# First 192 rows' local scaling shared by two engines, and a new searched order table

## The chip, the cores and the metric

One core of one Trainium2 chip runs one program that holds the whole chain. The metric is the device time in microseconds, the median of several executions. Lower is better.

## What is computed

The input has 4 batches of 8 heads, 576 rows and 64 columns. Attention is the sum of two parts, each a softmax of its own: one over means of 4 rows, repeated back to full length, and one over neighbours less than 4 rows away. Its output, as 2304 rows of 512, goes through two experts.

```
out_up = repeat(softmax(q_d k_d^T / 8) v_d, 4)         # q_d, k_d, v_d: means of 4 rows
attn   = out_up + softmax(where(|i-j| < 4, q k^T / 8, -1e9)) v
h = x @ w_in;  x1 = (max(h, 0) + alpha * min(h, 0)) @ w_out        # 512 -> 2048 -> 512
xn = x1 / rms(x1) * rms_g
out = (silu(xn @ w_gate) * (xn @ w_val)) @ w_out2                  # 512 -> 1536 -> 512
```

Both softmaxes divide by their sum plus 1e-9. All is fp32.

## The kernel before, in words

The large products take fp32 apart into a high and a low fp16 half and add three fp16 products on TensorE. The weights therefore go through a chain before use: a DMA on the SP queue brings a raw piece (L1143, L1153), ScalarE and VectorE decode it (`Piece.decode`, L1162, L1165, L1167, L1170, L1171), TensorE squares it (`sqps`, L1183), VectorE takes the sum of squares (L1184), TensorE adds it over the partitions (`allps`, L391), a few small VectorE steps make a power of two as scale (L404 to L408), and `split` writes the high half on ScalarE (L415) and the low half on VectorE (L416). For `w_in` the two halves stand in the tile `wi`; it comes in six pieces.

Batch 0's first 384 rows are computed by the class `Dense`, on blocks of 96 rows (i, two of them) and 96 + 6 keys, for two halves of a head pair (j). Per pair of lanes `local` has these steps: scores on TensorE (`lsps`, L920 to L932), maxima on VectorE (L938), in `s1` exponentials with their row sums on ScalarE (L952, one instruction for each i and j, 96 x 102), in `s2` the inverse of the sums on VectorE (L958, L959) and the scaling of the exponentials (L967 on ScalarE for the first 192 rows, c = 0; GpSimd for the others, `self.big(c)`), in `s3` transposes on TensorE (`ltps`, L976) and their eviction on ScalarE (L978), in `s4` the products with v (`lops`, L988), the sum with the pooled part on VectorE (L997) and the split into `xt`. The pooled attention's steps in `down` are transposes `tps` (L844), their eviction `T` (L845), scores `sps`, exponentials `dd` (L877) and products `avps`.

The first expert for these rows is `m1_first`. It calls `h_mm` (L1416) for two column blocks of 128 at a time: 24 matmuls of 128 x 192 into one PSUM tile `hps`. There are two such buffers (`ps_w`, tag "w"). To empty one, ScalarE takes the negative part (L1420, tile `g`), VectorE adds it with its factor (L1422, twice), ScalarE writes the high half of the result (L415, tile `g0`), and VectorE the low half (L416). Only then is the buffer free for the next but one product. `hps_835`, `hps_921` and `hps_1008` are the first three.

```
        nc.scalar.activation(out=g, in_=ps, func=AF.Relu, scale=-1.0)
        for j in range(fs):
            nc.vector.scalar_tensor_tensor(out=ps[:, j], in0=g[:, j], scalar=oma[:, f + j:f + j + 1], in1=ps[:, j],
                                           op0=ALU.mult, op1=ALU.add)
```

The order on each engine is not that of the code. `issue_order` (from L72) is called last. It records all instructions with estimated costs (`cost`, `transfer`, `lag`), takes a list scheduler back and forth over them for 40 rounds, and keeps the best round's priorities. To these it adds the table `LEADS` (L24): each entry shifts the priorities of a range of instruction numbers by some ns. One more pass of the scheduler gives the sequence of every engine, which is then pinned as it stands. Its forward pass has a model of TensorE's clock: in stretches in which TensorE did little in the stretch before, its matmuls take about twice as long (`slow`). SP's DMA issues are an engine like the others there, so its queue is ordered by the same pass.

Of the kernel before, what the change touches and what calls it, by code (L numbers as in the profile page):

```python
# [12 lines left out]
AF = mybir.ActivationFunctionType  # L13
ALU = mybir.AluOpType
# [4 lines left out]
def view(ap, dims, off=0, parts=None):  # L19
# [2 lines left out]


LEADS = (  # L24
# [28 lines left out]
)  # L53


def issue_order(tc, nc, groups, rounds=40):
# [53 lines left out]
    def transfer(o, i):  # L110
        sides = [[c for _, c in a.ap if c > 1] or [1] for a in (o, i)]
        rings = max(x for x in range(1, 17) if not any(s[0] % x for s in sides))
        n = max(runs(a)[0] for a in (o, i))
        each = 4.0 * min(runs(a)[1] for a in (o, i))
        share = n / 16 * (10.0 + 0.046 * each)
        return max(share, n / rings * (9.0 + 0.042 * each)), max(share, 600.0)

    def cost(k, ins, outs):
        i, e = insts[k], eng[k]
# [61 lines left out]
    for k, (ins, outs) in enumerate(aps):  # L181
        for l, wr in ((ins, False), (outs, True)):
            for a in l:
                n = a.tensor.name
# [46 lines left out]
    def lag(a, b):  # L231
        return 2300 if eng[a] == "SP" else waits.get((eng[a], eng[b]), 100)
# [7 lines left out]
    def run(P, S, prio, fwd, d):  # L240
# [9 lines left out]
        for _ in count:  # L250
            t, e = min((clock[e] if now[e] else max(clock[e], soon[e][0][0]), e) for e in engines if now[e] or soon[e])
            while soon[e] and soon[e][0][0] <= t:
                k = heapq.heappop(soon[e])[1]
                heapq.heappush(now[e], (prio[k], k))
            k = heapq.heappop(now[e])[1]
            if fwd and e == "PE":
                while t >= (win + 1) * WIN:
                    slow, win, done = done < BUSY, win + 1, 0
                done += work[k]
                real[k] = (2 * d[k] - 2.5 if slow else d[k]) + fixed[k]  # L260
            if fwd and shared[k]:
                real[k] += max(0.0, port - t)
                port = t + real[k]
            end[k] = t + real[k]
            clock[e] = end[k] if held[k] is None else t + held[k]
            seq[e].append(k)
            for s in S[k]:
                left[s] -= 1
                at[s] = max(at[s], end[k] + (lag(k, s) if fwd else lag(s, k)))
                if not left[s]:  # L270
                    if fwd and mate.get(k) == s:
                        heapq.heappush(now[e], (-1e30, s))
                    else:
                        heapq.heappush(soon[eng[s]], (at[s], s))
# [22 lines left out]
def kernel(  # L297
# [14 lines left out]
    nc = tc.nc  # L312
# [458 lines left out]
    class Dense:  # L771
# [141 lines left out]
        def local(self, c, h0, banks):  # L913
# [42 lines left out]
            def s2():  # L956
# [3 lines left out]
                for n, s in enumerate(ls["s"]):  # L960
# [2 lines left out]
                                                op=ALU.mult)  # L963
                        continue
                    for i in range(QC):
                        for j in range(2):
                            nc.scalar.activation(out=s[:, i, j], in_=s[:, i, j], func=AF.Copy,  # L967
                                                 scale=sm[:, n, i, j:j + 1])

            def s3():  # L970
                ls["t"] = []
# [819 lines left out]
```

## Time and profile before

| | us |
|---|---|
| median of 3 runs (lowest, highest) | 958.61 (958.48, 958.99) |
| profiled execution | 958.69 |
| its span | 957.0 |
| TensorE (PE) busy | 928.3 (97%) |
| VectorE (DVE) busy | 676.8 (71%) |
| ScalarE (ACT) busy | 481.4 (50%) |
| GpSimd (POOL) busy | 128.0 (13%) |

The span reaches from the first to the last instruction that the profiler saw; the execution's own time has 1.7 us around it. Busy is the time in which an engine's instructions ran; TensorE's loading of weights (PEld) lies beside its matmuls. An arrow in a row names what the engine waited for: `[0.73 <-DVE g L416]` is idle time of 0.73 us before the instruction, ended by VectorE's work on tile g at line 416. Names of tiles carry a number only in the listings of the order.

### The profile page before, as it was taken

Reading aid. Unit: us, or ns where it says so; the run is one execution under the profiler, and the core shown is the slowest. Engines: PE = TensorE matmul, PEld = TensorE weight load, DVE = VectorE, ACT = ScalarE, POOL = GpSimd, SP = SyncE. Lnnn points to the kernel's source line nnn. Section 1 sums busy time; section 2 is a strip of 40 time slices with the busy share of each in tenths; the row PEclk is TensorE's granted clock in tenths of the full one; section 3 lists DMA queues with packets and bytes.
Section 4 is the critical chain, followed back from the end, with each engine's and each line's share of the span. In section 5 each row is a group of like instructions: output and inputs, shape, how many; then the busy total and the mean of one; then the engine's idle time right before and its main releaser. Section 6 shows DMA issues by size and latency. Waiting matters only on the chain.

```text
span 957.0 us, 16449 instructions
## 1 busy us (share of the span) xinstructions
PE 928.3 (97%) x6484; PEld 599.6 (63%) x6484; DVE 676.8 (71%) x1333; ACT 481.4 (50%) x1108; POOL 128.0 (13%) x103
## 2 busy tenths in 40 slices
PE   6978999999999999999999999999999999999998
PEld 5667877799555565556666655555566666555554
DVE  4789996899999968999977899973333342442333
ACT  5899989889872472233576322222332433221322
POOL 1101100211022003332102323220000000000000
PEclk9999999999999999999999999999999999999999
DMA  9976444574221241121032120200000000000000
GB/s 214 278 253 177 130 143 130 196 234 137 72 74 58 91 150 50 55 78 55 25 88 84 50 65 20 50 18 1 23 12 1 1 2 1 1 1 12 23 1 34
DMA packets 53711, 73.79 MB, mean 77 GB/s; under 512 B 22190, under 2 KB 35138, under 8 KB 53634
## 3 DMA queue, kind: packets, MB, share of 16 engines
q1 hardware_dynamic: 53634, 72.74, 25.3%
q8 instruction: 51, 0.84, 0.4%
q14 instruction: 26, 0.21, 0.1%
HBM read 68.01 MB, written 4.72 MB: 76 GB/s over the span
## 4 chain that ended last, share of the span: by engine, by line
PE 78%; ACT 4%; DMA 3%; DVE 3%; issue 1%; SPq 0%; ACTq 0%
PE gps L1533 26%; PE acc L1433 16%; PE hps L1416 16%; PE oacc L1562 14%; DMA out_dram<-ob 3%; PE avps L749 1%; PE sps L709 1%; PE atps L737 1%; DMA wr<-in_moe_w_gate_dram 1%; ACT wr L1165 1%; ACT w L415 1%; DVE prod L575 1%; PE xps L612 1%; DVE hps L1422 1%; DVE wc L1167 0%
## 5 line engine op out<-in xcount | busy, mean ns | idle before, releaser
L1416 PE MATMUL hps<-xt,wi 128*128 128x192 f16 (+1 forms) x1536 | 345.9, 289 | 6.6 <-DVE g L416 4.3
L1533 PE MATMUL gps<-x,w 128*128 128x384 f16 x1728 | 349.5, 326 | 0.6 <-ACT x L1447 0.4
L1433 PE MATMUL acc<-ghl,wo 128*128 128x384 f16 (+1 forms) x960 | 249.4, 310 | 0.5 <-ACT ghl L415 0.4
L1533 PEld LDWEIGHTS <-w 128*128 128x128 f16 x1728 | 169.4, 98 | 116.5 <-issue 2.6
L1562 PE MATMUL oacc<-w,uhl 128*128 128x512 f16 x630 | 200.4, 379 | 1.8 <-ACT ob L1618 1.7
L1416 PEld LDWEIGHTS <-wi 128*128 128x128 f16 x1536 | 148.0, 100 | 59.3 <-issue 7.7
L1433 PEld LDWEIGHTS <-wo 128*128 128x128 f16 x1344 | 128.8, 99 | 60.0 <-issue 2.6
L1422 DVE SCALAR_TENSOR_TENSOR hps<-g,oma,hps 128x192 f32<-128x192 f32 (+1 forms) x128 | 66.1, 517 | 66.1 <-ACT g L1420 65.4
L1542 ACT ACTIVATE th<-gps,tsc 128x384 f32<-128x384 f32 x72 | 41.7, 581 | 124.2 <-PE gps L1533 123.9
L1562 PEld LDWEIGHTS <-uhl 128*128 128x128 f16 x630 | 61.8, 98 | 64.3 <-issue 2.5
L1544 DVE SCALAR_TENSOR_TENSOR th<-th,gps 128x384 f32<-128x384 f32 x72 | 39.6, 551 | 84.9 <-ACT th L1542 84.7
L1553 ACT ACTIVATE uhl<-gps 128x384 f16<-128x384 f32 x72 | 41.7, 579 | 107.0 <-DVE gps L1547 98.5
L1420 ACT ACTIVATE g<-hps 128x384 f32<-128x384 f32 x96 | 47.0, 489 | 95.7 <-PE hps L1416 95.4
L521 POOL TENSOR_TENSOR prod<-cq,ckv 128x896 f32<-128x896 f32 x24 | 53.1, 2213 | 172.9 <-DVE ls L532 52.2
L1433 PE MATMUL acc<-g,wo 128*128 128x384 f16 (+1 forms) x384 | 69.8, 286 | 0.0
L1554 DVE TENSOR_TENSOR uhl<-gps,uhl 128x384 f16<-128x384 f32 x72 | 45.4, 630 | 28.4 <-ACT uhl L1553 28.1
L575 POOL TENSOR_TENSOR prod<-ls,ckv 128x896 f32<-128x896 f32 x24 | 47.9, 1997 | 126.4 <-issue 54.8
L416 DVE SCALAR_TENSOR_TENSOR ghl<-hps,grp,ghl 128x384 f16<-128x384 f32 (+1 forms) x73 | 44.3, 608 | 27.0 <-ACT ghl L415 26.7
L415 ACT ACTIVATE ghl<-hps,grp 128x384 f16<-128x384 f32 (+1 forms) x73 | 41.9, 574 | 40.2 <-DVE hps L1422 37.2
L532 DVE TENSOR_REDUCE ls<-prod 128x14 f32<-128x896 f32 x48 | 51.0, 1076 | 0.0
L1162 ACT ACTIVATE wr<-wr 128x768 f32<-128x768 f32 (+1 forms) x48 | 41.5, 874 | 8.7 <-DMA wr<-in_moe_w_val_dram 4.9
L1547 DVE SCALAR_TENSOR_TENSOR gps<-th,kap,gps 128x384 f32<-128x384 f32 x60 | 37.1, 618 | 9.6 <-PE gps L1533 7.0
(240 smaller groups left out, 1143.4 us busy)
## 6 DMA issues: line engine op xcount, KB each, us to landing
wr<-in_moe_w_out_dram SPq DMA_DIRECT2D x18, 512.0 KB
wr<-in_moe_w_in_dram SPq DMA_DIRECT2D x10, 768.0 KB
wr<-in_moe_w_gate_dram SPq DMA_DIRECT2D x8, 768.0 KB
wr<-in_moe_w_val_dram SPq DMA_DIRECT2D x8, 768.0 KB
ckv<-in_k_dram SPq DMA_DIRECT2D x7, 768.0 KB
ckv<-in_v_dram SPq DMA_DIRECT2D x7, 768.0 KB
wr<-in_moe_w_out_dram SPq DMA_DIRECT2D x20, 256.0 KB
sd<-in_q_dram SPq DMA_DIRECT2D x24, 144.0 KB
```

The source lines that it names most:

```text
L415: nc.scalar.activation(out=hi, in_=src, func=AF.Copy, scale=s)
L416: nc.vector.scalar_tensor_tensor(out=lo, in0=src, scalar=s, in1=hi, op0=ALU.mult, op1=ALU.subtract)
L521: engs[i].tensor_tensor(out=pr, in0=view(st["q"][:, j, t:t + TP], [[D, TP], [0, ND], [1, D]]), in1=view(st["k"][:, j, t:t + TP], [[D, TP], ...
L532: nc.vector.tensor_reduce(out=st["s"][:, j, t:t + TP], in_=st.pop(("p", i)), axis=AX.X, op=ALU.add)
L575: engs[i].tensor_tensor(out=over(pr, i), in0=view(st["s"][:, j, t:t + TP], [[ND, TP], [1, ND], [0, D]]), in1=view(st["v"][:, j, t:t + TP], ...
L1416: nc.tensor.matmul(ps[:, j], wi[:, f + j, a, kk * 128:(kk + 1) * 128], x[:, b_, kk, c0:c0 + n], start=(i == 0), stop=(i == 3 * KK - 1))
L1420: nc.scalar.activation(out=g, in_=ps, func=AF.Relu, scale=-1.0)
L1422: nc.vector.scalar_tensor_tensor(out=ps[:, j], in0=g[:, j], scalar=oma[:, f + j:f + j + 1], in1=ps[:, j], op0=ALU.mult, op1=ALU.add)
L1433: nc.tensor.matmul(acc[e], wo_f(f)[:, a, e * 128:(e + 1) * 128], hl[:, b_], start=(f == f0 and i == 0), stop=(f == f1 and i == 2))
L1533: nc.tensor.matmul(ps, w2_t[i0 + f // 3].rearrange("p a (k c) -> p a k c", k=KK)[:, a, kk, (f % 3) * 128:(f % 3 + 1) * 128], xh[:, b_, kk] ...
L1554: nc.vector.tensor_tensor(out=t1, in0=vp, in1=t0, op=ALU.subtract)
L1562: nc.tensor.matmul(acc[tt], t[:, a, tt * 128:(tt + 1) * 128], w[:, b_, f % 3], start=(f in first and i == 0), stop=(f in last and i == 2))
```

## The change

Three parts. In `s2` the first 192 rows' exponentials were scaled by ScalarE alone, 16 instructions of 96 x 102; now j = 0 stays on ScalarE and j = 1 is scaled by VectorE. In the planner, a transfer of at most 16 runs costs at least 3000 ns in its model, and in its slow stretches a matmul that finds TensorE idle costs 90 ns more and its followers on other engines come 100 ns later. And the table `LEADS` holds other entries, three rows fewer (its first row before and now is shown). Lines of the changed kernel from L256 on stand up to 4 lower or higher than before; the scalings are L967 and L968, and other lines named below are one higher from there on (L1420 is L1421).

```
 LEADS = (
-    (6142, 6149, 8500), (4634, 4657, 4000), (1841, 1850, 500), (2437, 2444, -500), (1116, 1482, 1000), (6896, 6972, -500),
...
+    (6142, 6149, 8500), (5545, 5548, 22500), (2175, 2183, 4500), (493, 561, -3000), (3639, 3651, -19500), (450, 467, -3500),
...
@@ -113,7 +110,7 @@
         n = max(runs(a)[0] for a in (o, i))
         each = 4.0 * min(runs(a)[1] for a in (o, i))
         share = n / 16 * (10.0 + 0.046 * each)
-        return max(share, n / rings * (9.0 + 0.042 * each)), max(share, 600.0)
+        return max(share, n / rings * (9.0 + 0.042 * each), 3000.0 if n <= 16 else 0.0), max(share, 600.0)
 
     def cost(k, ins, outs):
         i, e = insts[k], eng[k]
@@ -253,11 +250,15 @@
                 k = heapq.heappop(soon[e])[1]
                 heapq.heappush(now[e], (prio[k], k))
             k = heapq.heappop(now[e])[1]
+            late = 0.0
             if fwd and e == "PE":
                 while t >= (win + 1) * WIN:
                     slow, win, done = done < BUSY, win + 1, 0
                 done += work[k]
                 real[k] = (2 * d[k] - 2.5 if slow else d[k]) + fixed[k]
+                if slow:
+                    real[k] += 90.0 if t > clock[e] else 0.0
+                    late = 100.0
             if fwd and shared[k]:
                 real[k] += max(0.0, port - t)
                 port = t + real[k]
@@ -266,7 +267,7 @@
             seq[e].append(k)
             for s in S[k]:
                 left[s] -= 1
-                at[s] = max(at[s], end[k] + (lag(k, s) if fwd else lag(s, k)))
+                at[s] = max(at[s], end[k] + late + (lag(k, s) if fwd else lag(s, k)))
                 if not left[s]:
                     if fwd and mate.get(k) == s:
                         heapq.heappush(now[e], (-1e30, s))
@@ -963,9 +964,9 @@
                                                 op=ALU.mult)
                         continue
                     for i in range(QC):
-                        for j in range(2):
-                            nc.scalar.activation(out=s[:, i, j], in_=s[:, i, j], func=AF.Copy,
-                                                 scale=sm[:, n, i, j:j + 1])
+                        nc.scalar.activation(out=s[:, i, 0], in_=s[:, i, 0], func=AF.Copy, scale=sm[:, n, i, 0:1])
+                        nc.vector.tensor_scalar(out=s[:, i, 1], in0=s[:, i, 1], scalar1=sm[:, n, i, 1:2],
+                                                scalar2=None, op0=ALU.mult)
 
             def s3():
                 ls["t"] = []
```

Three places of the order. The first is the scaling of the first lanes. On ScalarE it stood thus before (`dls` are the exponentials, `dlsum` the sums; `dd` are exponentials of the pooled part):

```order
L877 ACTIVATE dd_334,dsum_344<-sps_337,dm_343 72x144
L877 ACTIVATE dd_334,dsum_344<-sps_338,dm_343 72x144
L877 ACTIVATE dd_334,dsum_344<-sps_337,dm_343 72x144
L877 ACTIVATE dd_334,dsum_344<-sps_338,dm_343 72x144
L967 ACTIVATE dls_414<-dls_414,dlsum_411 96x102 x2
L967 ACTIVATE dls_419<-dls_419,dlsum_411 96x102 x2
L1165 ACTIVATE wr_665<-wr_665,nhalf_99 128x768
L845 ACTIVATE T0_200<-tps_363 128x288
```

and stands thus with the change:

```order
L878 ACTIVATE dd_334,dsum_344<-sps_338,dm_343 72x144
L1166 ACTIVATE wr_690<-wr_690,nhalf_99 128x768
L878 ACTIVATE dd_334,dsum_344<-sps_337,dm_343 72x144
L967 ACTIVATE dls_414<-dls_414,dlsum_411 96x102
L878 ACTIVATE dd_334,dsum_344<-sps_338,dm_343 72x144
L967 ACTIVATE dls_419<-dls_419,dlsum_411 96x102
L967 ACTIVATE dls_414<-dls_414,dlsum_411 96x102
L967 ACTIVATE dls_419<-dls_419,dlsum_411 96x102
```

with this on VectorE:

```order
L862 TENSOR_TENSOR dd_316<-sdv_160 72x256
L960 RECIPROCAL dlsum_411<-dlsum_411 96x8
L650 SCALAR_TENSOR_TENSOR vqps_236,vm_225<-vqps_236,ident_97 128x128
L968 TENSOR_SCALAR dls_414<-dls_414,dlsum_411 96x102
L968 TENSOR_SCALAR dls_419<-dls_419,dlsum_411 96x102
L968 TENSOR_SCALAR dls_414<-dls_414,dlsum_411 96x102
L968 TENSOR_SCALAR dls_419<-dls_419,dlsum_411 96x102
L860 TENSOR_TENSOR sdv_166<-sdv_166 72x4x128
```

The four scalings of j = 1 are a row on VectorE, right behind the inverse of the sums, between sums of squares and the pooled means of v (`sdv`, `dd`).

The second is ScalarE's queue up to the first high halves (`g0_834<-hps_835`). Before, with nine weight splits in a row:

```order
L1162 ACTIVATE wr_768<-wr_768 128x768
L415 ACTIVATE wi_107<-wc_662,swi_113 128x512 x3
L415 ACTIVATE wi_107<-wc_687,swi_113 128x512 x3
L415 ACTIVATE wi_107<-wc_712,swi_113 128x512 x3
L1162 ACTIVATE wr_1108<-wr_1108 128x768
L1420 ACTIVATE g_860<-hps_835 128x384
L1165 ACTIVATE wr_1108<-wr_1108,nhalf_99 128x768
L1420 ACTIVATE g_946<-hps_921 128x384
L1162 ACTIVATE wr_770<-wr_770 128x768
L415 ACTIVATE g0_834<-hps_835,sc_105 128x2x192
```

With the change:

```order
L416 ACTIVATE wi_107<-wc_687,swi_113 128x512 x2
L1163 ACTIVATE wr_1184<-wr_1184 128x768
L416 ACTIVATE wi_107<-wc_712,swi_113 128x512
L1166 ACTIVATE wr_1184<-wr_1184,nhalf_99 128x768
L416 ACTIVATE wi_107<-wc_742,swi_113 128x512 x2
L1421 ACTIVATE g_860<-hps_835 128x384
L416 ACTIVATE wi_107<-wc_767,swi_113 128x512
L416 ACTIVATE wi_107<-wc_742,swi_113 128x512
L1421 ACTIVATE g_946<-hps_921 128x384
L416 ACTIVATE g0_834<-hps_835,sc_105 128x2x192
```

The same instruction is row 110 before and row 137 with the change (a row may stand for several), and pieces of the weights from 742 and 767, which before were decoded and split behind it, are split in front of it.

The third is SP's queue of loads, near its start. Before:

```order
L1143 DMA wr_665<-in_moe_w_in_dram 128x2x768
L795 DMA wo_108<-in_q_dram 96x6x64
L803 DMA sdv_166<-in_v_dram 72x2x512
L795 DMA wo_108<-in_k_dram 96x6x64
L803 DMA sdv_172<-in_v_dram 72x2x512
L803 DMA sdv_174<-in_v_dram 72x2x512
L795 DMA wo_108<-in_q_dram 96x6x64
L795 DMA wo_108<-in_k_dram 96x6x64
```

With the change:

```order
L796 DMA wo_108<-in_k_dram 96x6x64
L804 DMA sdv_160<-in_v_dram 72x2x512
L796 DMA wo_108<-in_k_dram 96x6x64
L1144 DMA wr_665<-in_moe_w_in_dram 128x2x768
L796 DMA wo_108<-in_q_dram 96x6x64
L1696 DMA rows_176<-in_moe_alpha_dram 16x128
L1696 DMA rows_176<-in_moe2_rms_g_dram 4x128
L796 DMA wo_108<-in_q_dram 96x6x64
L796 DMA wo_108<-in_k_dram 96x6x64
L1144 DMA wr_688<-in_moe_w_in_dram 128x2x768
```

The loads of the third head's q and k (`wo` from `in_q` and `in_k`, in the second half of these pieces) stand ahead of three loads of v (`sdv_166`, `sdv_172`, `sdv_174`), and the second and third weight pieces (`wr_665`, `wr_688`) have fewer loads ahead of them.

## Rows read from the trace of the kernel before

**Rows 1.** The page: its head and part 1, busy time by engine.
```profile
span 957.0 us, 16449 instructions
...
PE 928.3 (97%) x6484; PEld 599.6 (63%) x6484; DVE 676.8 (71%) x1333; ACT 481.4 (50%) x1108; POOL 128.0 (13%) x103
```

**Rows 2.** Busy time by stretch: start:end length, engines, granted clock, DMA share, GB/s.
```profile
0.00:40.00 40.00, 30.89 (x197) 23.52 (x197) 23.28 (x74) 26.71 (x83) 5.82 (x30) 1.00 1.00 248
40.00:80.00 40.00, 33.86 (x286) 27.00 (x283) 33.33 (x79) 37.87 (x103) 1.46 (x2) 0.91 0.80 264
80.00:120.00 40.00, 36.53 (x448) 31.15 (x445) 38.15 (x107) 37.80 (x114) 8.09 (x12) 1.00 0.44 119
120.00:160.00 40.00, 40.00 (x400) 31.38 (x398) 33.27 (x87) 36.68 (x94) 0.00 (x0) 1.00 0.45 130
...
240.00:250.00 10.00, 7.95 (x61) 5.46 (x61) 9.08 (x17) 7.77 (x11) 1.84 (x1) 1.00 0.15 50
```

**Rows 3.** Busy time by stretch: columns PE, PEld, DVE, ACT, POOL as above.
```profile
0.00:21.10 21.10, 13.38 (x76) 9.73 (x77) 9.36 (x37) 10.08 (x35) 3.23 (x28) 1.00 0.95 209
...
0.00:71.60 71.60, 57.72 (x412) 44.08 (x413) 49.65 (x131) 56.19 (x154) 7.10 (x31) 0.98 0.89 248
...
72.30:107.70 35.40, 31.68 (x375) 27.82 (x375) 33.14 (x93) 33.20 (x101) 3.99 (x8) 0.95 0.57 156
```

**Rows 4.** TensorE's waits, 0 to 120 us: us in total, times, longest.
```profile
PE hps L1416 <- DVE g L416: 4.3, 4, 2.5
```

**Rows 5.** Timeline of TensorE: start, us, line, operation, tiles, shape, count, idle before.
```profile
72.30 0.90 PE L1416 MATMUL hps<-xt,wi 128*128 128x192 f16 x9 [2.47 <-DVE g L416]
...
105.43 1.40 PE L1416 MATMUL hps<-xt,wi 128*128 128x192 f16 x15 [0.73 <-DVE g L416]
...
107.40 2.90 PE L1416 MATMUL hps<-xt,wi 128*128 128x192 f16 x33
```

**Rows 6.** Timeline of ScalarE, first high halves.
```profile
71.02 0.57 ACT L415 ACTIVATE g<-hps,sc 128x384 f16<-128x384 f32 x1
```

**Rows 7.** Timeline of VectorE, first and ninth low halves.
```profile
71.62 0.62 DVE L416 SCALAR_TENSOR_TENSOR g<-hps,sc,g 128x384 f16<-128x384 f32 x1
...
107.05 0.61 DVE L416 SCALAR_TENSOR_TENSOR g<-hps,sc,g 128x384 f16<-128x384 f32 x1
```

**Rows 8.** Timeline of ScalarE, two exponentials of one row and four scalings.
```profile
19.01 0.33 ACT L952 ACTIVATE dls<-lsps,dlm 96x102 f32<-96x102 f32 x1
...
19.33 0.33 ACT L952 ACTIVATE dls<-lsps,dlm 96x102 f32<-96x102 f32 x1
...
24.46 1.20 ACT L967 ACTIVATE dls<-dls,dlsum 96x102 f32<-96x102 f32 x4
```

**Rows 9.** Groups of ScalarE, 0 to 71.6 us, shapes apart: count, busy us, mean ns, idle.
```profile
L1162 ACT ACTIVATE wr<-wr 128x768 f32<-128x768 f32 x15 | 13.5, 905 | 1.9 <-DMA wr<-in_moe_w_in_dram 1.7
L1165 ACT ACTIVATE wr<-wr,nhalf 128x768 int32<-128x768 uint32 x9 | 8.9, 991 | 0.0
...
L415 ACT ACTIVATE wi<-wc,swi 128x512 f16<-128x512 f32 x9 | 5.6, 709 | 0.3 <-DVE swi L406 0.3
L967 ACT ACTIVATE dls<-dls,dlsum 96x102 f32<-96x102 f32 x16 | 5.4, 381 | 0.0
...
L978 ACT ACTIVATE laT<-ltps 102x384 f32<-102x384 f32 x4 | 1.9, 485 | 0.0
...
L1162 ACT ACTIVATE wr<-wr 128x256 f32<-128x256 f32 x1 | 0.4, 434 | 0.0
```

**Rows 10.** Groups of VectorE, 0 to 107.7 us, shapes apart.
```profile
L1170 DVE TENSOR_SCALAR wc<-wr 128x768 int32<-128x768 int32 x6 | 3.3, 549 | 1.4 <-ACT wr L1162 1.4
...
L1170 DVE TENSOR_SCALAR wc<-wr 128x256 int32<-128x256 int32 x2 | 0.6, 292 | 0.3 <-ACT wr L1162 0.3
```

**Rows 11.** Busy time by stretch: columns as above, the granted clock third from last.
```profile
66.00:67.00 1.00, 1.00 (x8) 0.92 (x7) 1.00 (x3) 1.00 (x3) 0.00 (x0) 0.50 1.03 365
...
76.00:77.00 1.00, 1.00 (x9) 0.95 (x7) 1.00 (x3) 1.00 (x8) 0.00 (x0) 0.50 1.03 321
```

More of the change, by code (lines that the diff above doesn't have):

```diff
@@ L115, in transfer @@
         share = n / 16 * (10.0 + 0.046 * each)
-        return max(share, n / rings * (9.0 + 0.042 * each)), max(share, 600.0)
+        return max(share, n / rings * (9.0 + 0.042 * each), 3000.0 if n <= 16 else 0.0), max(share, 600.0)
     def cost(k, ins, outs):
@@ L255, in run @@
             k = heapq.heappop(now[e])[1]
+            late = 0.0
             if fwd and e == "PE":
@@ L260, in run @@
                 real[k] = (2 * d[k] - 2.5 if slow else d[k]) + fixed[k]
+                if slow:
+                    real[k] += 90.0 if t > clock[e] else 0.0
+                    late = 100.0
             if fwd and shared[k]:
@@ L268, in run @@
                 left[s] -= 1
-                at[s] = max(at[s], end[k] + (lag(k, s) if fwd else lag(s, k)))
+                at[s] = max(at[s], end[k] + late + (lag(k, s) if fwd else lag(s, k)))
                 if not left[s]:
@@ L965, in s2 @@
                     for i in range(QC):
-                        for j in range(2):
-                            nc.scalar.activation(out=s[:, i, j], in_=s[:, i, j], func=AF.Copy,
-                                                 scale=sm[:, n, i, j:j + 1])
+                        nc.scalar.activation(out=s[:, i, 0], in_=s[:, i, 0], func=AF.Copy, scale=sm[:, n, i, 0:1])
+                        nc.vector.tensor_scalar(out=s[:, i, 1], in0=s[:, i, 1], scalar1=sm[:, n, i, 1:2],
+                                                scalar2=None, op0=ALU.mult)
             def s3():
```

53 rows, old and new, of the table LEADS are left out of this document.

## The prediction

> **What bounds the kernel now.** I read the page's head, then the busy time by stretch, then what the engines wait for in the first 120 us, and last the single rows around the first expert's h products. TensorE is busy for 928.3 of 957.0 us [rows 1], so at most 28.7 us can be had from waits, and the stretches say where they lie. The three of 40 us up to 120 us hold 30.89, 33.86 and 36.53 us of TensorE work, which leaves 9.1 + 6.1 + 3.5 = 18.7 us idle; from 120 to 160 us nothing is idle, and the 10 us from 240 on hold 7.95, so 2.05 are lost there [rows 2]. The change touches none of the matmuls' sizes and its moves end at some 320 us. So it works on these 20.8 us.
>
> In the head the weights and the attention of batch 0 are made ready together. ScalarE is then busy for 56.19 of the first 71.60 us, idle for 15.4, and 11.0 of that idle time had passed by 21.10 us (10.08 busy), while TensorE waited for its inputs [rows 3]. From then on ScalarE works almost without a gap, in a fixed order. What TensorE waits for most often once the h products begin is the release of their PSUM buffers: 4.3 us in 4 waits [rows 4]. There are two such buffers; the third product waits 2.47 us, to 72.30, for the first pair's values, and later ones 0.73 us [rows 5]. The values come out by way of ScalarE, then VectorE: the high halves of the first product start on ScalarE at 71.02 [rows 6], the low halves on VectorE at 71.62, done at 72.2; the ninth product's low halves start at 107.05 and are done at 107.7 [rows 7], and tile hps_1514, the eleventh product, reuses that buffer. It starts some 0.1 us later, within the run of 33 matmuls from 107.40 [rows 5]. Between the two low halves VectorE is busy for 33.14 of 35.40 us [rows 3]. So two queues in series set when TensorE gets on here: ScalarE up to the first high half, VectorE from there to the ninth low half.
>
> **The change, part by part.**
>
> *Scalings.* Of 16 on ScalarE, 8 stay and 8 go to VectorE. Four in a row take 1.20 us [rows 8], 0.38 of it one alone [rows 9], so each costs 0.27 by its distance to the next: 8 x 0.27 = 2.2 us less for ScalarE. VectorE's price for 96x102 is not in the trace. Its nearest rows are the same kind of operation on 256 elements, 0.292 us, and on 768, 0.549 [rows 10]; the smaller width can cost no more than the first and no less than nothing beyond its fixed part, which a line through both puts at 0.292 - 256 x 0.0005 = 0.16. I take 0.22, on that line, so 8 x 0.22 = 1.8 us, bounds 1.3 to 2.3. VectorE is idle for 71.6 - 49.65 = 22.0 us ahead of the first product's values [rows 3], and that covers it. The Trainium skill (VectorE: DVE Perf Modes, Mode 2×_2P) says that a one-source fp32 operation from SBUF to SBUF reads through both ports and yields two results a cycle; the slope between the two rows, 0.0005 us an element, agrees with it.
>
> *ScalarE ahead of the first high halves.* The new order puts 142 instructions ahead of them where 122 stood. By kind, at the distance from one to the next (an instruction's recorded time less the some 0.11 us by which it overlaps its follower): 16 more exponentials at 0.32 [rows 8] = 5.1; 4 more weight splits at 0.61 = 2.4; 2 more decodings of 768 at 0.80 and 2 of 256 at 0.32 = 2.2; 2 more of the other decoding at 0.88 = 1.8; 2 more evictions of transposes at 0.37 = 0.7 [rows 9]; 8 fewer scalings, -2.2. Sum 10.0 us, so 56.2 + 10.0 = 66.2 us of ScalarE work in place of 56.2. Its idle time has a floor of 11.0 us, already past by 21.10 us [rows 3]; loads that come earlier (the third head's keys, the second weight piece) can lower the 4.4 us that came later, and weight pieces wanted earlier than their loads can raise it, by 1.9 us if the last one is waited for. I take 15.4, as it was. The first high halves are then done at 66.2 + 15.4 = 81.6 and the low halves 0.6 later, at 82.2 instead of 72.2: 10.0 us later. VectorE is not the later one: its rows ahead of that point rise by some 9 us, to 59 us of work, with 22 us to spare.
>
> *VectorE from the first to the ninth low half.* 87 rows stand there where 83 stood. Five decoding steps, two joinings of the output weights, two weight splits and three square sums go out; adds and reductions of the pooled attention and two sums of the local one come in; by the durations in the trace both weigh the same, 33.2 and 33.3 us. With 0 to 2.3 us of idle time (2.3 before), taken at 1.1, hps_1514 starts at 82.2 + 33.3 + 1.1 = 116.6 in place of 107.8: 8.8 us later.
>
> *TensorE's work ahead of it.* More of it is done by then: 16 transposes, 16 local products, 8 of the pooled attention's squares, 8 transposes and 4 products of it, 4 of h, 2 of the output. At the distances in the trace (0.09, 0.06, 0.07, 0.09, 0.15, 0.085, 0.16 us) that is 5 us, and 5.5 with the slower spacing where kinds alternate. So of 8.8 us 5.5 are paid back: +3.3 us.
>
> *Clock.* Before shows whole microseconds at 0.50 of the full clock, 1.2 of 2.4 GHz, while h products run [rows 11]; there are two such stretches of 3.4 us, each costing 1.7 us of TensorE. While the two queues above set the time, the clock costs nothing beyond what they allow, and I put it at nothing. Later TensorE does not stand long enough to show a fall in the rows of before.
>
> *Queues.* GpSimd's order is untouched. On SP the loads of the third head pass three loads of v, and weight pieces move ahead; the effect is in the idle time above. The 2.05 us at 240 us [rows 2] rest on an order that changes too; between nothing and all of it can go, and I take 1.0.
>
> *Sum.* +3.3 - 1.0 = +2.3 us. The profiled execution took 958.69 (span 957.0 and 1.7 around it), which is 0.1 over the median of the three runs. 958.7 + 2.3 = 961.0.
>
> *Ends.* Low: ScalarE idle 13.0, no idle time on VectorE, all of 2.05 back: 79.8 + 33.3 = 113.1, +5.3 - 5.5 - 2.05 = -2.3, so 956.4. High: idle 17.3, VectorE idle 2.3, nothing back: 84.1 + 35.6 = 119.7, +11.9 - 5.5 = +6.4, so 965.1.
>
> **The rivals.**
>
> *Faster: the head's loads decide, not the queues.* If the reordered loads take away ScalarE's late idle time down to the floor of 11.0 us, the first low halves are done at 77.8 and hps_1514 at 111.1: +3.3 - 5.5 = -2.2, and with the wait at 240 us gone, -4.3: 954.4 to 956.5. It decides from an idle time of some 13 us downwards. For it: 4.4 us of waiting after 21 us, and the third head's loads moved up. Against it: the weight pieces are wanted earlier too, from the same DMA.
>
> *No change.* The added work ahead is the same work that came behind, and TensorE uses the wait: with ScalarE idle at 14 us and no idle time on VectorE the sum is 80.8 + 33.3 = 114.1, +6.3 - 5.5 - 1.0 = -0.2: 958.5. The scaling's 2.2 us are in it. That the shared scaling alone changes nothing is part of this case: it frees ScalarE inside a chain that other work fills.
>
> *Slower by more: the clock falls again.* TensorE now waits longer ahead of the first buffers, and twice the clock has been at 0.50 beside such a wait [rows 5, 11]. If after hps_1514, where TensorE is the bound again, two more such stretches follow, 2 x 1.7 us are added: 964.4. The Trainium skill (TensorE: Matmul & The Clock Gate, A second HAM failure mode: psum-queue depth-cycling) describes the same: small idle spells between groups of matmuls as PSUM buffers go round make the clock swing; it speaks against an order that bunches the waits. The half-clock rows of before agree with it, but after 80 us the clock reads 1.00 [rows 2].
>
> **How the numbers follow.** A measurement of this kernel can tell about 0.2%, 1.9 us, from no change. The forecast of about 961 I give 0.38, the clock rival 0.10, no change 0.28, faster 0.24. The forecast's own range is 960.0 to 963.5. Slower by over 1.9 us: 0.38 + 0.10 = 0.48; within: 0.28; faster: 0.24. The range for 8 in 10 goes from 956.0 to 965.1: it leaves out some two thirds of the faster case and the end of the clock case.
>
> **What would show it.** Right: first high halves on ScalarE near 81 us, first low halves near 82, the ninth's near 116; ScalarE's idle time up to there near 15.4; eight scalings of 0.2 to 0.3 us on VectorE within time it had free; nothing idle on TensorE from 120 to 160 us. Wrong: first low halves before 79 us, or hps_1514 before 113, or waits gone after 160 us by more than 2 us; then the gain came from loads or from later stages that this sum holds still.

## The result, and the profile after

| | before | changed |
|---|---|---|
| median of 6 runs, us (lowest, highest) | 959.74 (958.48, 961.64) | 967.74 (966.77, 969.87) |
| ratio to before, 95% interval | | 1.0083 [1.0063, 1.0103] |
| profiled execution, us (span) | 958.69 (957.0) | 967.33 (965.6) |
| TensorE idle, 0 to 160 us | 18.7 | 21.9 |
| TensorE idle, 160 to 240 us | 0.1 | 0.2 |
| TensorE idle, 240 to 640 us | 3.6 | 9.0 |
| TensorE idle after 640 us | 6.3 | 6.4 |

The change makes the kernel 8.0 us slower by the medians, 8.6 by the two profiles. TensorE's work is the same, to 0.1 us; the page's head and its first part for the changed kernel:

```profile
span 965.6 us, 16449 instructions
...
PE 928.2 (96%) x6484; PEld 600.6 (62%) x6484; DVE 671.3 (70%) x1341; ACT 477.6 (49%) x1100; POOL 128.0 (13%) x103
```

So the whole loss is idle time of TensorE, and the stretches say where it lies. Busy time by stretch of the changed kernel (start:end length, then PE, PEld, DVE, ACT, POOL, granted clock, DMA share, GB/s; the first four answer to [rows 2]):

```profile
0.00:40.00 40.00, 27.52 (x179) 22.27 (x181) 24.69 (x77) 25.40 (x75) 4.86 (x29) 1.00 1.01 252
40.00:80.00 40.00, 34.02 (x277) 26.29 (x274) 31.30 (x81) 37.13 (x110) 6.11 (x6) 0.91 0.77 239
80.00:120.00 40.00, 36.53 (x441) 30.98 (x439) 38.74 (x108) 35.19 (x103) 3.84 (x8) 1.00 0.55 165
120.00:160.00 40.00, 40.00 (x396) 31.40 (x395) 33.23 (x86) 37.77 (x98) 0.00 (x0) 1.00 0.43 125
240.00:280.00 40.00, 36.72 (x265) 24.70 (x263) 38.13 (x75) 32.42 (x48) 4.90 (x3) 1.00 0.31 99
320.00:400.00 80.00, 78.25 (x501) 44.80 (x499) 68.50 (x130) 35.62 (x111) 15.21 (x7) 1.00 0.29 89
400.00:640.00 240.00, 236.04 (x1476) 142.03 (x1475) 212.05 (x383) 95.44 (x233) 63.45 (x33) 1.00 0.19 58
```

Up to 160 us 3.2 us are lost against before (40 - 27.52 = 12.5 idle in place of 9.1 in the first 40 us, the rest alike). From 240 to 640 us 5.4 us are lost: 3.3 against 2.2 up to 280, 1.8 against 0.4 from 320 to 400, 4.0 against 1.1 from 400 to 640.

The first low halves come later than forecast, the ninth's near the forecast. ScalarE's busy time up to the first low halves, same columns, answers to [rows 3]:

```profile
0.00:83.52 83.52, 64.60 (x488) 51.09 (x489) 59.46 (x163) 66.05 (x190) 11.11 (x37) 0.96 0.89 249
```

83.52 - 66.05 = 17.5 us of idle time on ScalarE, 15.4 before. The first and the ninth low halves on VectorE, from its timeline, answer to [rows 7]:

```profile
83.52 0.62 DVE L417 SCALAR_TENSOR_TENSOR g<-hps,sc,g 128x384 f16<-128x384 f32 x1
...
116.74 0.61 DVE L417 SCALAR_TENSOR_TENSOR g<-hps,sc,g 128x384 f16<-128x384 f32 x1
```

They start 11.9 and 9.7 us later than before. And the eight scalings on VectorE take 0.27 us each (shortest, median, longest in ns, from the instructions of line 968):

```profile
L968 DVE TENSOR_SCALAR dls<-dls,dlsum x8: 259/266/268, 26.5 to 58.0; 96x102 f32<-96x102 f32 x8
```

What TensorE waits for in the head is another thing than before. The waits for the buffers' release [rows 4] fall to 1.4 us, and in the first 40 us a wait for loads of v is new; these loads stand further back in SP's queue now. From the waits of 0 to 120 us (us in total, times, longest):

```profile
PE vqps L649 <- DMA sdv<-in_v_dram: 2.0, 1, 2.0
PE hps L1417 <- DVE g L417: 1.4, 2, 0.7
```

The last wait of the h products for a buffer ends at 91.30 us; from there to 160 us TensorE stands for no more than 0.33 us at a time, so the ninth low halves do not hold it here.

The later waits of TensorE, one row each from its timeline (in brackets the idle time and what ended it); before had none of over 0.51 us from 243 to 640 us:

```profile
249.56 0.32 PE L1534 MATMUL gps<-x,w 128*128 128x384 f16 x1 [1.71 <-DVE ghl L417]
...
275.71 0.32 PE L1534 MATMUL gps<-x,w 128*128 128x384 f16 x1 [0.95 <-DVE uhl L1555]
...
361.93 0.65 PE L1534 MATMUL gps<-x,w 128*128 128x384 f16 x3 [0.94 <-DVE th L1545]
...
404.43 0.39 PE L1563 MATMUL oacc<-w,uhl 128*128 128x512 f16 x1 [1.19 <-ACT uhl L1554]
...
435.66 0.32 PE L1417 MATMUL hps<-xt,wi 128*128 128x384 f16 x1 [1.30 <-DVE ghl L417]
```

They sum to 6.1 us. All five are ended by VectorE, or by ScalarE right behind VectorE. In each case VectorE ran a long row shortly ahead of what is awaited. These are the rows for four of the five (the fifth is another of 1.81 us, at 273.39):

```profile
247.18 1.81 DVE L417 SCALAR_TENSOR_TENSOR w<-wc,sw,w 128x1536 f16<-128x1536 f32 x1
...
358.96 2.19 DVE L687 TENSOR_TENSOR dd<-sd 72x256 f32<-72x256 f32 x1
...
400.44 2.79 DVE L522 TENSOR_TENSOR prod<-cq,ckv 128x896 f32<-128x896 f32 x1
...
432.35 2.73 DVE L576 TENSOR_TENSOR prod<-ls,ckv 128x896 f32<-128x896 f32 x1
```

The three others are TENSOR_TENSOR operations with two inputs from SBUF; most rows of the same form take 1.08 us (128x896) and 0.42 us (72x256) in this trace. GpSimd's timeline has a product at the same time:

```profile
358.43 2.44 POOL L522 TENSOR_TENSOR prod<-cq,ckv 128x896 f32<-128x896 f32 x1 [39.58 <-DVE dm L716]
...
400.21 2.08 POOL L522 TENSOR_TENSOR prod<-cq,ckv 128x896 f32<-128x896 f32 x1 [3.68 <-DVE lo L592]
...
432.05 2.08 POOL L522 TENSOR_TENSOR prod<-cq,ckv 128x896 f32<-128x896 f32 x1 [4.29 <-DVE lo L592]
```

358.43 + 2.44 = 360.87, 400.21 + 2.08 = 402.29, 432.05 + 2.08 = 434.13: VectorE's operation, begun during GpSimd's, ends 0.28, 0.94 and 0.95 us after that end (361.15, 403.23, 435.08), about its own length, so it stood still until then. The Trainium skill (SBUF — State Buffer, Who interferes with whom) has this as a rule: a VectorE instruction with two SBUF inputs and a GpSimd instruction that reads SBUF exclude each other, and the later one waits for the whole of the earlier. The rows agree.

Such holds are not new. Before had such products beside GpSimd's, as long and at much the same times, and TensorE had no wait over 0.51 us there; two rows of VectorE's timeline before:

```profile
395.52 2.73 DVE L521 TENSOR_TENSOR prod<-cq,ckv 128x896 f32<-128x896 f32 x1
...
432.23 2.96 DVE L521 TENSOR_TENSOR prod<-cq,ckv 128x896 f32<-128x896 f32 x1
```

So a hold by itself does not make TensorE wait; it matters what stands behind it in VectorE's queue.

### The profile page after: what moved, and what is told of

It is laid out like the page before. It is cut to its first block, busy times and chain, and to the rows that moved or that the text cites. A ratio compares the mean times of both kernels' runs of the same rounds, so it can differ in the third digit from the quotient of the medians.

```text
span 965.6 us, 16449 instructions
## 1 busy us (share of the span) xinstructions
PE 928.2 (96%) x6484; PEld 600.6 (62%) x6484; DVE 671.3 (70%) x1341; ACT 477.6 (49%) x1100; POOL 128.0 (13%) x103
## 4 chain that ended last, share of the span: by engine, by line
PE 75%; DVE 9%; ACT 7%; DMA 6%; issue 2%; SPq 0%; ACTq 0%; DVEq 0%
PE gps L1534 26%; PE hps L1417 15%; PE acc L1434 15%; PE oacc L1563 13%; DMA out_dram<-ob 3%; DMA wo<-in_q_dram 2%; DVE prod L576 1%; ACT wr L1163 1%; ACT dls L953 1%; DVE hps L1423 1%; DMA wr<-in_moe_w_out_dram 1%; ACT wr L1166 1%; PE avps L750 1%; ACT wi L416 1%; PE sps L710 1%
## 5 line engine op out<-in xcount | busy, mean ns | idle before, releaser
L1534 PE MATMUL gps<-x,w 128*128 128x384 f16 x1728 | 343.3, 326 | 4.7 <-DVE ghl L417 2.0
L1417 PE MATMUL hps<-xt,wi 128*128 128x192 f16 (+1 forms) x1536 | 334.7, 287 | 3.0 <-DVE g L417 1.4
L1563 PE MATMUL oacc<-w,uhl 128*128 128x512 f16 x630 | 193.8, 379 | 3.0 <-ACT ob L1619 1.8
L1417 PEld LDWEIGHTS <-wi 128*128 128x128 f16 x1536 | 145.3, 99 | 53.5 <-issue 3.1
L1421 ACT ACTIVATE g<-hps 128x384 f32<-128x384 f32 x96 | 47.3, 494 | 84.5 <-PE hps L1417 84.5
L522 POOL TENSOR_TENSOR prod<-cq,ckv 128x896 f32<-128x896 f32 x24 | 55.3, 2304 | 170.1 <-DVE ls L533 62.9
L1434 PE MATMUL acc<-g,wo 128*128 128x192 f16 (+1 forms) x384 | 66.8, 286 | 0.1
```

Of the source, the lines that this page charges most:

```text
L522: engs[i].tensor_tensor(out=pr, in0=view(st["q"][:, j, t:t + TP], [[D, TP], [0, ND], [1, D]]), in1=view(st["k"][:, j, t:t + TP], [[D, TP], ...
L1417: nc.tensor.matmul(ps[:, j], wi[:, f + j, a, kk * 128:(kk + 1) * 128], x[:, b_, kk, c0:c0 + n], start=(i == 0), stop=(i == 3 * KK - 1))
L1434: nc.tensor.matmul(acc[e], wo_f(f)[:, a, e * 128:(e + 1) * 128], hl[:, b_], start=(f == f0 and i == 0), stop=(f == f1 and i == 2))
L1534: nc.tensor.matmul(ps, w2_t[i0 + f // 3].rearrange("p a (k c) -> p a k c", k=KK)[:, a, kk, (f % 3) * 128:(f % 3 + 1) * 128], xh[:, b_, kk] ...
L1563: nc.tensor.matmul(acc[tt], t[:, a, tt * 128:(tt + 1) * 128], w[:, b_, f % 3], start=(f in first and i == 0), stop=(f in last and i == 2))
```

## The experiments

Orders are pinned in all of them, so an edit moves what it names and nothing else. "New" is the changed kernel's order, "old" that of before. Idle time is TensorE's, in the profiled execution, whose own time can lie some us off the median. The lines of most of these kernels stand up to 70 lower than those of the changed kernel.

| | median us | ratio to before [95%] | profiled us | idle 0-160 | 160-240 | 240-640 |
|---|---|---|---|---|---|---|
| scaling alone | 958.97 | 0.9998 [0.9979, 1.0018] | 960.36 | 19.4 | 0.4 | 3.6 |
| order alone | 969.06 | 1.0103 [1.0073, 1.0133] | 968.87 | 24.9 | 0.0 | 9.0 |
| new to 150, then old | 965.82 | 1.0076 [1.0049, 1.0104] | 966.28 | 26.2 | 0.8 | 3.5 |
| old to 150, then new | 974.48 | 1.0159 [1.0129, 1.0189] | 975.85 | 21.5 | 7.5 | 8.6 |
| five moves | 969.27 | 1.0100 [1.0063, 1.0137] | 972.04 | 28.8 | 0.0 | 8.1 |
| more ScalarE work | 964.73 | 1.0058 [1.0040, 1.0076] | 964.70 | 23.7 | 0.4 | 3.5 |
| more VectorE work | 965.48 | 1.0055 [1.0034, 1.0077] | 967.08 | 22.6 | 0.8 | 3.6 |
| new to 310, then old | 964.71 | 1.0038 [1.0019, 1.0056] | 965.74 | 22.8 | 0.5 | 5.1 |
| old to 310, then new | 964.40 | 1.0050 [1.0023, 1.0078] | 961.99 | 17.5 | 1.2 | 7.0 |
| changed again | 968.75 | 1.0083 [1.0052, 1.0115] | 972.38 | 28.6 | 0.0 | 8.2 |
| 31 moves | 975.85 | 1.0192 [1.0168, 1.0216] | 971.76 | 21.6 | 0.0 | 12.2 |

**The two parts apart.** The scaling alone, in the old order, which was planned as if all 16 stood on ScalarE:

```
-    nc.scalar.activation(out=s[:, i, j], ...)                     # j = 0 and 1
+    nc.scalar.activation(out=s[:, i, 0], ...)
+    nc.vector.tensor_scalar(out=s[:, i, 1], ...)
+    # after the plan: the 8 of j = 1 go from ScalarE's sequence to VectorE's, by their planned start
```

> The order of the kernel before on every engine, only the 8 scalings of j = 1 taken out of ScalarE's queue and put into VectorE's, each at the place where it was due. Theory (head set by two queues, scaling worth 2.2 us of ScalarE in a chain): up to 2.2 us faster than before, 956.5 to 958.7 by the profiled time. Rival (the scaling's share is hidden by other waits): within 0.5 us of before. A price on VectorE near 0.22 us each in both.

Measured 958.97 against 959.16, ratio 0.9998: no change, though the interval reaches from 2.0 us faster to 1.7 us slower, so a part of the theory's 2.2 us is not excluded. ScalarE's busy time up to the first low halves, which start at 72.49 in this run:

```profile
0.00:72.49 72.49, 57.92 (x412) 44.54 (x413) 50.96 (x139) 54.48 (x146) 7.26 (x31) 0.98 0.88 249
```

It is 1.7 us less than before (54.48 for 56.19), but the idle time is 18.0 for 15.4. In this execution what was taken off ScalarE became waiting. One execution cannot show that it always does: with the same order up to 310 us (below) the idle time was 14.2 us, and the low halves started at 68.64. The medians are nearer to the rival. The order alone is the reverse edit on the changed kernel.

> The changed kernel's order on every engine, only the 8 scalings of j = 1 put back into ScalarE's queue where they were due. Theory: the loss is in the order, so 967 to 969.5 (up to 2.2 us over the changed kernel). Rival (VectorE's scalings delay what stands behind them in its queue and cause the loss): near 959.

969.06, ratio 1.0103. The whole loss is there without VectorE's scalings, so it is the order's.

**Where in the order.** Both plans are made in one kernel and joined: what one plan starts before a given time (with all that it depends on) keeps that plan's sequence on every engine, the rest follows in the other's.

```
+    head = those that the first plan starts before 150e3 (later: 310e3) ns, and all before them
-    best = the plan's sequence
+    best = {e: [k for k in seq[e] if k in head] + [k for k in rest[e] if k not in head] for e in seq}
```

> The new order for everything that the planner starts before 150 us, and behind it the order of the kernel before. Theory 1 (the head loses 3.2 us by its queues, and the new later order loses 5.4 us by its own waits): 961.5 to 962.5, with the waits of the changed kernel at 250, 276, 325, 362, 404 and 436 us gone. Theory 2 (the later waits are knocked on by the late head): near 967, with these waits still there.

> The order of the kernel before for everything that its planner starts before 150 us (with the scalings on both engines), and the new order behind it. Theory 1 (the later order loses by itself): 963 to 965, with waits in TensorE from 240 to 640 us of some 10 us in all. Theory 2 (waits are knocked on by the late head): 958 to 959.5.

965.82 lies between the two theories, 974.48 over both, since the join costs: 1.35 us of idle time from 120 to 160 us in the first, and in the second one wait of 8.30 us. (The head of the first, 26.2 us idle, is also a bad one; see the changed kernel's second run below.) But the later waits decide. TensorE's timeline of the second, old head and new tail:

```profile
167.50 1.00 PE L1001 MATMUL lsps<-T 64*96 64x102 f32 x8 [8.30 <-ACT T L1114]
...
258.22 0.32 PE L1602 MATMUL gps<-x,w 128*128 128x384 f16 x1 [1.72 <-DVE ghl L485]
...
413.09 0.39 PE L1631 MATMUL oacc<-w,uhl 128*128 128x512 f16 x1 [1.19 <-ACT uhl L1622]
```

The 1.71 and 1.19 us of the changed kernel are back as 1.72 and 1.19, behind the old head, and so are the three others, as 0.94, 0.94 and 1.30. With the old order behind the new head none of the five is there, and 240 to 640 us hold 3.5 us, as before. So the later waits belong to the later order. A join at 310 us, where little is under way, gives the parts without that cost.

> The new order for all that the planner starts before 310 us, behind it the order of the kernel before; the orders join where little is under way, so that the join itself should cost TensorE at most 1.5 us. Theory 1 (the two halves lose by themselves): the waits near 249 and 276 us are there, those of the changed kernel from 325 to 440 us are gone; the head's 2.6 to 4.9 us and about 1 us up to 280 us remain: 963 to 966. Theory 2 (what comes late in the head makes the later waits): as the changed kernel.

> The order of the kernel before (the scalings on both engines) for all that the planner starts before 310 us, behind it the new order. Theory 1: head as before, the waits of the changed kernel from 325 to 440 us there, each within 0.1 us of its length, 4.3 us of TensorE idle more than before from 320 to 640 us: 962.5 to 964.5. Theory 2: as before, within 1.5 us.

New up to 310 us: 4.4 us slower than before. Its timeline has the two waits of 249 and 276 us and then the old 0.51:

```profile
251.77 0.32 PE L1602 MATMUL gps<-x,w 128*128 128x384 f16 x1 [1.72 <-DVE ghl L485]
...
277.93 0.32 PE L1602 MATMUL gps<-x,w 128*128 128x384 f16 x1 [0.95 <-DVE uhl L1623]
...
430.09 0.97 PE L1485 MATMUL hps<-xt,wi 128*128 128x384 f16 x5 [0.51 <-DVE ghl L485]
```

Old up to 310 us: 4.1 us slower, and these are its waits, 0.94, 1.19 and 1.30 as in the changed kernel:

```profile
356.56 0.65 PE L1602 MATMUL gps<-x,w 128*128 128x384 f16 x3 [0.94 <-DVE th L1613]
...
399.06 0.39 PE L1631 MATMUL oacc<-w,uhl 128*128 128x512 f16 x1 [1.19 <-ACT uhl L1622]
...
430.30 0.32 PE L1485 MATMUL hps<-xt,wi 128*128 128x384 f16 x1 [1.30 <-DVE ghl L485]
```

By the ratios' intervals the two halves lose 1.8 to 5.4 and 2.2 to 7.5 us. 4.4 + 4.1 = 8.5, and the changed kernel beside them is 8.45 slower: the halves add up as closely as these intervals can tell, and both came out in theory 1's range, with its waits. Of the first half's 4.4 us, 1.5 are in 240 to 640 us (5.1 for 3.6); some 2.9 are left for the head.

**The head's two queues.** More work for each, in the old order:

```
+    if f < 8: nc.scalar.activation(out=w[:, 0], in_=c, func=AF.Copy, scale=...)      # ahead of split's, same values
     split(w[:, 0], w[:, 1], c, ...)
```

> The kernel before, its order kept, with eight of the nine weight splits ahead of the first h product done twice on ScalarE (the same values written again): 8 x 0.62 = 5.0 us more for ScalarE right ahead of the first high halves. Theory (ScalarE's queue up to the first high halves, then VectorE's, set the head): first low halves 5 us later, 77 us, the ninth's near 112.5, 3 to 5 us slower. Rival (loads and TensorE's waits of the first 40 us set the head, and ScalarE has slack): under 1.5 us slower.

4.9 us slower. The low halves start 5.5 and 5.7 us later (71.62 and 107.05 before):

```profile
77.14 0.61 DVE L426 SCALAR_TENSOR_TENSOR g<-hps,sc,g 128x384 f16<-128x384 f32 x1
...
112.71 0.61 DVE L426 SCALAR_TENSOR_TENSOR g<-hps,sc,g 128x384 f16<-128x384 f32 x1
```

```
     split(hl[:, :, 0], hl[:, :, 1], ps, col(S_AL))
+    nc.vector.scalar_tensor_tensor(out=hl[:, :, 1], in0=ps, scalar=col(S_AL), in1=hl[:, :, 0], ...)   # again
```

> The kernel before, its order kept, with the low halves of the second to the ninth product written twice by VectorE: 8 x 0.53 = 4.2 us more between the first and the ninth low halves, where VectorE was idle for 2.3 us. Theory: the ninth's low halves 2 to 4.2 us later, and 1.5 to 4.2 us slower. Rival: hidden by other work, under 1 us slower.

5.6 us slower (3.3 to 7.4 by the interval), over the 1.5 to 4.2 expected. From the first low halves to the ninth it took 40.0 us (69.60 to 109.58) for 35.4. Beyond that TensorE has a new wait, and the granted clock from 80 to 160 us is 0.96 where it was 1.00:

```profile
125.43 0.71 PE L719 MATMUL sps<-qkT 64*72 64x144 f32 x8 [2.46 <-ACT qkT L709]
```

In the old order both queues are on the path: 5.0 us put on ScalarE's cost 4.9, and 4.2 put on VectorE's cost 5.6, of which the new wait and the clock make a part. For the new order no run tests it.

**VectorE's place in the later waits.** Five moves in VectorE's sequence of the changed kernel, and nothing else:

```
+    for at, to in ((480, 479), (529, 528), (682, 679), (737, 736), (790, 789)):
+        move instruction at of VectorE's sequence in front of instruction to
```

> The changed kernel with five moves in VectorE's order and nothing else: at 249, 276, 361, 404 and 436 us the instruction that TensorE waits for goes in front of the long one that stands right before it (1.81, 1.81, 2.19, 2.79 and 2.73 us). Theory (VectorE's place of these instructions, and GpSimd holding VectorE up at three of them, makes the 6.1 us of waits): these five waits gone, 4.5 to 6.1 us faster than the changed kernel, 962 to 963.5. A moved long instruction that then starts later while GpSimd still works is shorter by as much. Rival (VectorE is short of time there and the waits come back behind): within 2 us of the changed kernel.

The median did not fall: 969.27, and the changed kernel had 967.74 and 968.75 in two other sets of runs. Idle from 240 to 640 us is 8.1 us, the changed kernel's 8.2 to 9.0. The five waits are gone or shorter, and others stand in their place:

```profile
256.71 0.38 PE L399 MATMUL allps<-s,ones 128*128 128x1 f32 x2 [2.09 <-ACT w L1184]
...
368.50 0.26 PE L745 MATMUL atps<-ident,dd 72*72 72x72 f32 x1 [1.14 <-ACT dd L736]
...
448.37 0.48 PE L1424 MATMUL hps<-xt,wi 128*128 128x384 f16 x2 [0.63 <-DVE ghl L424]
```

The rival holds. GpSimd's hold is borne out by the same run, with VectorE's two products and GpSimd's beside them:

```profile
407.06 2.07 DVE L529 TENSOR_TENSOR prod<-cq,ckv 128x896 f32<-128x896 f32 x1
...
438.88 1.45 DVE L583 TENSOR_TENSOR prod<-ls,ckv 128x896 f32<-128x896 f32 x1
```

```profile
406.10 2.08 POOL L529 TENSOR_TENSOR prod<-cq,ckv 128x896 f32<-128x896 f32 x1 [3.68 <-DVE lo L599]
...
437.30 2.08 POOL L529 TENSOR_TENSOR prod<-cq,ckv 128x896 f32<-128x896 f32 x1 [4.28 <-DVE lo L599]
```

Begun 0.96 and 1.58 us after GpSimd's, they take 2.07 and 1.45 us, where 2.79 and 2.73 had begun 0.23 and 0.30 after: each ends 0.95 us after GpSimd's end.

31 such moves, each time what empties a PSUM buffer past work of the pooled attention, by the order of ready times in the changed kernel's trace:

```
+    for at, to in ((480, 479), (529, 528), (624, 621), ... 31 in all, to 640 us):
+        move instruction at of VectorE's sequence in front of instruction to
```

> The changed kernel with 31 moves in VectorE's order from 249 to 640 us: each time the instruction that empties a PSUM buffer or feeds TensorE goes one to three places forward, past work of the pooled attention that ran although the other's input was there. Nothing else is changed. Theory (over this stretch VectorE's order, 2 to 5 us of other work too early, makes the waits): TensorE idle from 240 to 640 us falls from 8.2 to 9.0 us to 5 or less, near the 3.6 of before. Rival (the work that is passed over is itself waited for, as after the five moves): 7 us or more.

Worse: 975.85, and 12.2 us idle from 240 to 640 us in the fastest of the four executions, 971.76. Other waits stand where the old ones were, among them two for VectorE's `th`:

```profile
373.96 0.32 PE L1540 MATMUL gps<-x,w 128*128 128x384 f16 x1 [1.59 <-DVE th L1551]
...
554.04 2.27 PE L1540 MATMUL gps<-x,w 128*128 128x384 f16 x13 [1.48 <-DVE th L1551]
```

**The changed kernel again.**

> The changed kernel as it is, beside the two others on the same chip. 966.5 to 969.5; its idle time up to 120 us tells how far the head varies from one execution to the next, its waits from 240 to 640 us should come back within 0.1 us.

968.75. Of its later waits all but one come back within 0.1 us; that at 436 us is 0.49 here, 1.30 before. The head varies: its busy time up to 40 us and up to the first low halves, at 90.52 in this run, is

```profile
0.00:40.00 40.00, 21.18 (x128) 15.90 (x129) 20.14 (x64) 20.16 (x59) 4.38 (x29) 1.00 0.98 214
0.00:90.52 90.52, 64.45 (x488) 50.55 (x489) 60.38 (x164) 66.29 (x190) 10.63 (x37) 0.96 0.86 229
```

ScalarE idle 90.52 - 66.29 = 24.2 us, with loads at 214 GB/s in place of 252. TensorE waits longer for the loads of v, too:

```profile
PE vqps L649 <- DMA sdv<-in_v_dram: 6.4, 2, 4.6
```

This execution took 972.38, the longest of its five. Over the five profiled executions that have this head whole, TensorE was idle for 21.6 to 28.8 us up to 160 us, so the 3.2 us of the first profile are near the least that the head loses.

## Why the prediction was wrong

**The direction and the head.** The forecast put +3.3 us on the head, by ScalarE's queue up to the first high halves, VectorE's up to the ninth low halves, and TensorE's work done meanwhile. ScalarE's work came out at 66.05 us (66.2 forecast), the ninth low halves were done at 117.35 us (116.6), and the head lost 3.2 us in the profile. The medians less the idle time after 240 us leave it 2.6 us (8.0 - 5.4) and, in the second set of runs, 3.9 (8.45 - 4.6). That the sum came so near is in part luck. Two terms inside were off and nearly cancel: ScalarE's idle time was not 15.4 us as it was, but 17.5 to 24.2 in six executions of this head (13.4 to 18.3 in six of the old one), over my high end of 17.3 each time, because the weight pieces are wanted earlier than their loads (ScalarE waits for loads of `w_in` for 4.1 us in 4 waits, 1.7 before, and for 11.1 in a run with 24.2); and VectorE needed 33.2 us between the two low halves, for 34.4. And TensorE did not lose the time where the forecast had it, at the buffers, but in the first 40 us, among others on the loads of v that SP's new order puts back, which I gave no term of their own.

**The step that failed** is the one on the later stages: "The 2.05 us at 240 us [rows 2] rest on an order that changes too; between nothing and all of it can go, and I take 1.0", and before it that the change's "moves end at some 320 us" and that it "works on these 20.8 us". The moves do not end there. Compared row by row (operation, tiles, shapes), VectorE's timelines of the two kernels differ in every 40 us up to 600, and hardly behind; at 432 us before runs `prod<-cq,ckv` and the changed kernel `prod<-ls,ckv`, in the rows above. An order that moves can lose as well as gain, and I gave that term no loss. Measured it is +5.4 us (+4.6 in the second profile), not -1.0. The forecast was 2.3 us over before and the medians say 8.0: of the 5.7 us between, this term makes 6.4, and the head, 2.6 for 3.3, gives back the other 0.7, as near as single profiles can tell. The range's high end, 965.1, was built from the head's bounds alone, so it could not hold this.

Even for the stretch up to 320 us I read only the waits that before had there. In the stretches from 240 to 640 us that are shown above VectorE is busy for 38.13 + 68.50 + 212.05 = 318.7 of 360 us. Before it was busy for 322.9 us in the same three stretches, with 3.6 us of idle time of TensorE: what got worse is not the sum of work, but what stands behind what.

**The scalings.** 0.27 us each against 0.22, within the bounds; hidden, as forecast; and the 2.2 us that they take off ScalarE bring nothing that the medians show in the old order. In the new order the 8 on ScalarE go with 1.3 us more (969.06 and 967.74, in different sets of runs), which the intervals do not tell apart.

**The rivals.** The clock did not fall again: 80 to 160 us read 1.00. Faster and no change are excluded by the interval.

**What stays open.** That the later order loses by itself is shown, and that the waits sit in VectorE's queue, three of five behind a hold by GpSimd. Why it is so much worse as a whole is not: two attempts to mend it in VectorE's order alone moved the waits or made them worse. The order of the other engines may have a part in it; no run isolates it, and none takes GpSimd's products away from the three places. That the loads of v make the head's loss is read from the waits alone; no run puts them back in SP's old place.

## What to carry to other kernels

When a table or a planner reorders the work, look first how far the new order reaches, and do not price only the waits that are there: for every engine that is near full in the moved stretch, allow for new waits, here five of 0.9 to 1.7 us in 400 us. Time taken off an engine that waits for loads further on brought nothing measurable here; work put in front of the first use of a queue that runs almost without a gap cost about its whole length. Splitting a changed order in time, with the old order before or behind, tells quickly which stretch loses.

## What was not expected of the hardware

VectorE's operations with two inputs from SBUF stood still while a GpSimd product ran: an operation of 1.08 us took 2.79 when begun 0.23 us after GpSimd's, 2.07 when 0.96 after, 1.45 when 1.58 after. And the first 40 us differ from one execution to the next with the loads: with the same order TensorE was busy for 27.5 us of them at 252 GB/s and for 21.2 at 214; a third execution, at 250, had 25.9, so the rate alone does not tell it.

The granted clock reads 1.00 in the first 62 us of both kernels, yet the same squares of 128 columns run at two paces there, 0.12 and 0.07 us each; the first row is the changed kernel's, the second that of before:

```profile
59.25 2.66 PE L1184 MATMUL sqps<-wc 128*128 128x128 bf16 x23
...
57.62 1.27 PE L1183 MATMUL sqps<-wc 128*128 128x128 bf16 x17
```

So a 1.00 early in these profiles does not show that TensorE ran at its full pace, and the stretches at 0.50 need not be all of its slow time. What this costs in the head no run separates.
